# The first batch's root mean square: made compactly with tokens on partitions, spread by TensorE, its casts issued ahead of later weights' narrowing

## The chip, the core and the metric

The kernel runs on one core of one Trainium2 chip. The metric is the device time of one execution in microseconds (us). The engines are named as in the profile: PE is TensorE's matmul, PEld its weight load, DVE is VectorE, ACT is ScalarE, POOL is GpSimd, SP is SyncE.

## What is computed

Attention without a softmax, normalised by its root mean square, and two MLPs behind it. There are 8 batches, 8 heads, 576 tokens and 64 values per head; the MLPs are 512 wide with 2048 hidden values, on 4608 tokens.

```python
kv = np.einsum('bhsd,bhse->bhde', k, v)
out = np.einsum('bhsd,bhde->bhse', q, kv)
rms = np.sqrt(np.mean(out * out, axis=-1, keepdims=True) + 1e-06)
x = out / rms * g_norm            # then tokens by 512 values
h = x @ w_in;  g = 0 if h <= -1, h if h >= 1, else (h + 1)**2 / 4;  x = g @ w_out
h = x @ moe2_w_in;  g = max(h, 0)**2;  x = g @ moe2_w_out
```

## The kernel before

**Stages.** The tokens go through the first MLP in blocks of 512. The attention of the first batch (b = 0) has to come first, since nothing else can feed the first MLP; that of the later batches lies in hooks between the MLP's products. After the start TensorE works on the MLPs' products without a break to the end.

**Three products for one.** The MLPs' f32 operands are split into a rounded value and a rest, `split` (L185): a cast on ACT (the "hi") and a subtraction on DVE (the "lo"); `mm3` then makes three products. A weight tile arrives as raw words and is narrowed first, `narrow_w` (L217): one ACT operation (L224) and two DVE operations (L226, L227), then split by `split_w` (L231; L173 the cast, L187 the subtraction). The weights of the first hidden tiles, w1_0_f (in) and w1_1_f (out), are narrowed and split while the first batch's attention runs.

**The first batch's attention** treats two heads together, hp = 0 to 3, in plain f32, with a head's 64 values on 64 partitions and 576 tokens in two halves of 288:

- `kv_stage` (L396): 8 + 2 small products pkv, and two DVE copies of 64x64 to kv0 (L175).
- `t_first` (L414): q is transposed by PE into pt, and copied by DVE to qT (L175).
- `o_first` (L428): per half one product po = kv0 by qT; ACT squares it to y (L434); o = po times g, on ACT for one half (L165) and on DVE for the other (L167).
- `r_first` (L447): per half one product pr = ones by y, which puts the mean of a head's squares on all of its 64 partitions; then the reciprocal root on the full 128x576: ACT takes Ln (L455, two halves), Exp (L457) and a square (L181); DVE makes one Newton step (L441, two halves; L444) and multiplies with o (L445). POOL keeps the tokens over 512 (L464), and the rest is split into x1_0_hp (L173 on ACT, L187 on DVE).

`attention` (L522) puts these into slots of a list, and the main program goes through it by slot; `split_w` of the first six weight tiles is put in at slots SPLITS. `keep_warm` (L985) issues bf16 products of zeros, pwarm, that nothing reads. The framework's scheduler then orders the instructions by priority, which is the order in which they are written, and by what is ready.

**PSUM.** There are eight banks: two of ps_t ("at"), two of ps_h ("h"), four of ps_a ("acc0" to "acc3"). `bank` (L325) hands all eight out in turn to the first batch. Later the first MLP's ph takes "h" and its second product acc takes "acc".

**After it** the first MLP begins: `h_stage` makes ph1_0_f = w1_0_f by the four x1_0_c (12 matmuls of 128x512, L194), ACT and DVE turn ph into u and split it into gs (L571, L573), and acc follows two tiles later.

Of the kernel before, what the change touches and what calls it, by code (L numbers as in the profile page):

```python
# [44 lines left out]
    "o": "AD A A",  # L45
# [31 lines left out]
def linear_attention_rms_two_mlps(  # L77
# [12 lines left out]
    nc = tc.nc  # L90
# [80 lines left out]
    def copy(e, dst, src):  # L171
        if e is nc.scalar:
            e.copy(dst, src)  # L173
        elif e is nc.vector:
            e.tensor_copy(dst, src)  # L175
        else:
            scaled(e, dst, src, 1.0)
# [7 lines left out]
    def split(t, src, op, phase):  # L185
        copy(engine(op + "_hi", phase), t[:, 0, :], src)
        engine(op + "_lo", phase).tensor_tensor(  # L187
            t[:, 1, :], src, t[:, 0, :].bitcast(F32), ALU.subtract
        )

# [41 lines left out]
    def split_w(L, f, which):  # L232
# [7 lines left out]
        if which == 1 and f >= NF - TAIL:  # L240
            nc.sync.dma_start(wtd[f - (NF - TAIL)], t.rearrange("p a f -> p (a f)").bitcast(F32))

# [51 lines left out]
    def prep_split(which, i, n):  # L294
# [26 lines left out]
    banks = itertools.cycle(  # L321
        [(ps_t, "at")] * 2 + [(ps_h, "h")] * 2 + [(ps_a, f"acc{c}") for c in range(KD)]
    )

    def bank(b, name):  # L325

        pool, tag = next(banks) if b == 0 else (ps_t, "at")
        return pool.tile([P, TB], F32, tag=tag, name=name)

# [40 lines left out]
    def load_first():  # L370


        left = wp.tile([REM, 2, H, D], F32, tag="w0_3", name="kvr0")
        qr = wp.tile([REM, H, D], F32, tag="w1_3", name="qr0")
# [53 lines left out]
    def o_first(hp):  # L428
        qT = hl.pop((0, hp))
        y, o = scratch(hp, "y"), scratch(hp, "o")  # L430
        for half in range(2):
            ps = bank(0, f"po_0_{hp}_{half}")
# [13 lines left out]

    def r_first(hp):  # L447
        y, o = og.pop((0, hp))
        t = scratch(hp, "t")
        ms = []  # L450
        for half in range(2):
            ps = bank(0, f"pr_0_{hp}_{half}")
            m = ps[:, :U]
            nc.tensor.matmul(m, ones.bitcast(F32), y[:, half], start=True, stop=True)
            nc.scalar.activation(y[:, half], m, AF.Ln, bias=lnb, scale=LN_SCALE)  # L455
            ms.append(m)
        nc.scalar.activation(y, y, AF.Exp, bias=expb, scale=-0.5)  # L457
        square(engine("y", 0), t, y)
        for half in range(2):
            newton(t[:, half], ms[half])  # L460
        norm(t, y, o)
# [4 lines left out]
        split(x, t[:, :, :n], "x", 0)  # L466
# [451 lines left out]
    for n, (L, b) in enumerate(blocks):  # L918
# [20 lines left out]
        if n == 0:  # L939
# [3 lines left out]
            for i in range(NF - AHEAD):  # L943
                for w in range(2):
                    hook(n, i, w, split_w, 1, i + AHEAD, w)
# [32 lines left out]
    for f in range(1, 4):  # L978
# [30 lines left out]
    for i in range(2 * AHEAD):  # L1009
        first.setdefault(SPLITS[i], []).append((split_w, (1, i // 2, i % 2)))  # L1010
    for s in sorted(first):
        for f, a in first[s]:
            f(*a)
    for f in range(4, 6):
# [80 lines left out]
```

## Time and profile before

| what | us |
|---|---|
| median of three runs | 1603.74 (1602.43, 1603.74, 1603.84) |
| the profiled execution | 1603.82 |
| its span, first to last instruction | 1602.0 |
| what lies around the span | 1.82 |

The mean granted clock of TensorE over the span is 0.994 of full speed. In rows of the trace's timeline a row is one instruction or several alike on one engine: its start, the time from its start to its last end, the engine, the source line, out<-in, the shape and the count; in square brackets the idle time of that engine ahead of it, and what ended it. An f32 product is two passes of PE, and so two records; a product of split operands is one.

### The profile page before, as it was taken

Reading aid. Unit: us, or ns where it says so; the run is one execution under the profiler, and the core shown is the slowest. Engines: PE = TensorE matmul, PEld = TensorE weight load, DVE = VectorE, ACT = ScalarE, POOL = GpSimd, SP = SyncE. Lnnn points to the kernel's source line nnn. Section 1 sums busy time; section 2 is a strip of 40 time slices with the busy share of each in tenths; the row PEclk is TensorE's granted clock in tenths of the full one; section 3 lists DMA queues with packets and bytes.
Section 4 is the critical chain, followed back from the end, with each engine's and each line's share of the span. In section 5 each row is a group of like instructions: output and inputs, shape, how many; then the busy total and the mean of one; then the engine's idle time right before and its main releaser. Section 6 shows DMA issues by size and latency. Waiting matters only on the chain.

```text
span 1602.0 us, 21127 instructions
## 1 busy us (share of the span) xinstructions
PE 1582.5 (99%) x7528; PEld 1294.9 (81%) x7528; DVE 949.9 (59%) x1574; ACT 912.0 (57%) x1661; POOL 112.0 (7%) x105
## 2 busy tenths in 40 slices
PE   8899999999999999999999999999999999999998
PEld 5788888888888888888888888888888888888886
DVE  6896656666666575643244348754974496457522
ACT  5886757667666675754344466546645663664321
POOL 0000000000000000000000121012101300320000
PEclk8999999999999999999999999999999999999999
DMA  9936567576766747523141457586769676865783
GB/s 261 270 110 162 194 182 224 170 220 200 224 199 206 235 143 222 195 82 105 40 146 39 156 190 245 191 215 224 238 199 243 205 227 192 248 216 191 191 244 104
DMA packets 306969, 302.36 MB, mean 189 GB/s; under 512 B 195504, under 2 KB 248752, under 8 KB 306864
## 3 DMA queue, kind: packets, MB, share of 16 engines
q1 hardware_dynamic: 304880, 300.22, 61.5%
q8 instruction: 60, 0.98, 0.2%
q10 hardware_dynamic: 1984, 0.79, 0.2%
q14 instruction: 45, 0.37, 0.1%
HBM read 231.74 MB, written 69.21 MB: 188 GB/s over the span
## 4 chain that ended last, share of the span: by engine, by line
PE 72%; issue 15%; DVE 8%; DMA 2%; ACT 2%; POOL 1%; SPq 0%; DVEq 0%; POOLq 0%; ACTq 0%
PE acc L194 27%; PE ph L194 27%; PE ph L749 10%; PE po L749 4%; DVE t L694 3%; PE pkv L406 2%; DVE x L694 1%; PE po L194 1%; DMA xr<-x1d 1%; POOL t L810 1%; PE pr L505 1%; DVE g L839 1%; DVE xr L717 1%; DMA raw<-in_moe_w_in_dram 1%; POOL g L811 0%
## 5 line engine op out<-in xcount | busy, mean ns | idle before, releaser
L194 PE MATMUL ph<-x,w 128*128 128x512 f32 x1728 | 423.2, 393 | 5.2 <-DVE u L573 2.6
L194 PEld LDWEIGHTS ph<-x,w 128*128 128x128 f32 x1728 | 322.3, 189 | 73.3 <-DVE u L573 3.3
L749 PE MATMUL po<-t,ws 128*128 128x512 f32 x1344 | 307.4, 390 | 1.9 <-DVE t L694 1.9
L749 PE MATMUL ph<-x,ws 128*128 128x512 f32 x1344 | 306.5, 389 | 0.6 <-DVE e L794 0.6
L749 PEld LDWEIGHTS po<-t,ws 128*128 128x128 f32 x1344 | 251.5, 188 | 57.1 <-DVE t L694 5.1
L749 PEld LDWEIGHTS ph<-x,ws 128*128 128x128 f32 x1344 | 252.1, 188 | 54.1 <-DVE e L794 1.9
L194 PE MATMUL acc<-gs,w 128*128 128x512 f32 x1152 | 281.4, 391 | 0.0
L194 PEld LDWEIGHTS acc<-gs,w 128*128 128x128 f32 x1152 | 213.8, 188 | 43.5 <-ACT ev L605 0.2
L571 ACT ACTIVATE u<-ph,halfb 128x512 f32<-128x512 f32 x144 | 99.3, 690 | 196.7 <-PE ph L194 195.9
L573 DVE SCALAR_TENSOR_TENSOR u<-u,ph 128x512 f32<-128x512 f32 x144 | 98.6, 684 | 171.8 <-ACT u L181 171.3
L694 DVE TENSOR_TENSOR t<-g,t 128x512 fp32r<-128x512 f32 x192 | 134.9, 709 | 74.3 <-ACT t L173 72.3
L173 ACT CAST t<-g 128x512 fp32r<-128x512 f32 x192 | 116.5, 621 | 71.8 <-DVE t L694 51.6
L187 DVE TENSOR_TENSOR gs<-u,gs 128x512 fp32r<-128x512 f32 x160 | 110.3, 689 | 61.0 <-ACT gs L173 60.0
L173 ACT CAST gs<-u 128x512 fp32r<-128x512 f32 x160 | 99.5, 622 | 71.7 <-DVE u L573 55.3
L194 PE MATMUL acc<-gs,wt 128*128 128x512 f32 x576 | 139.4, 391 | 0.0
L194 PEld LDWEIGHTS acc<-gs,wt 128*128 128x128 f32 x576 | 106.8, 188 | 21.6
L802 DVE TENSOR_TENSOR h<-ph,e 128x512 f32<-128x512 f32 x96 | 66.1, 691 | 55.9 <-PE ph L749 50.2
L803 ACT ACTIVATE h<-h 128x512 f32<-128x512 f32 x96 | 60.5, 630 | 60.0 <-DVE h L802 56.0
L181 ACT ACTIVATE u<-u 128x512 f32<-128x512 f32 x144 | 91.0, 632 | 2.1
L810 POOL TENSOR_TENSOR t<-g 128x512 f32<-128x512 f32 x32 | 43.1, 1346 | 633.9 <-ACT g L804 353.3
L804 ACT ACTIVATE g<-h 128x512 f32<-128x512 f32 x128 | 80.9, 632 | 3.6
L794 DVE TENSOR_TENSOR e<-ph,e 128x512 f32<-128x512 f32 x64 | 43.4, 688 | 44.3 <-PE ph L749 43.3
(108 smaller groups left out, 1433.1 us busy)
## 6 DMA issues: line engine op xcount, KB each, us to landing
ws<-wsd SPq DMA_DIRECT2D x224, 512.0 KB, 3.6
wsd<-s SPq DMA_DIRECT2D x112, 256.0 KB, 3.7
wt<-wtd SPq DMA_DIRECT2D x48, 512.0 KB, 4.4
raw<-in_moe_w_in_dram SPq DMA_DIRECT2D x32, 512.0 KB, 6.0
raw<-in_moe_w_out_dram SPq DMA_DIRECT2D x32, 512.0 KB, 6.0
wcd<-s SPq DMA_DIRECT2D x32, 512.0 KB, 3.1
ws<-wcd SPq DMA_DIRECT2D x32, 512.0 KB, 3.6
x1d<-ev SPq DMA_DIRECT2D x36, 256.0 KB, 3.5
```

What stands on the lines that cost most here:

```text
L173: e.copy(dst, src)
L181: e.activation(dst, src, AF.Square)
L187: engine(op + "_lo", phase).tensor_tensor(t[:, 1, :], src, t[:, 0, :].bitcast(F32), ALU.subtract)
L194: nc.tensor.matmul(dst, wt(a), xt(c), start=first and n == 0, stop=last and n == 2)
L571: nc.scalar.activation(u, ps, AF.Relu, bias=halfb, scale=0.5)
L573: nc.vector.scalar_tensor_tensor(u, u, 1.0, ps, op0=ALU.min, op1=ALU.max)
L694: engine2(op + "_lo").tensor_tensor(t[:, 1, :], src, t[:, 0, :].bitcast(F32), ALU.subtract)
L749: nc.tensor.matmul(ps, wt(a), xt(c), start=first and n == 0 and i == 0, stop=last and n == len(lhs) - 1 and i == 2, skip_group_check=True,)
L802: nc.vector.tensor_tensor(h, bank, add, ALU.add)
L803: nc.scalar.activation(h, h, AF.Relu)
L804: nc.scalar.activation(g, h, AF.Square)
L810: engine2("t_sum").tensor_tensor(t1[k], b, a, ALU.subtract)
```

## The change

`r_first` no longer makes the reciprocal root on 128x576. It multiplies each 96 tokens of y, as the stationary operand, by two columns of ones, which gives the means with 96 tokens on partitions and 12 columns (2 halves of 3 groups of 2 heads), pm. Ln, Exp, the square and the Newton step run on 96x12. Then each column, broadcast to 64 columns as the stationary operand, is multiplied by the 96x96 identity, which spreads it over 64 partitions, pr: 12 products for a pair of heads. DVE multiplies o by pr directly out of PSUM, per half. Three bf16 products of zeros are added per pair. o is made by ACT in both halves. po takes the "acc" banks, and the turn of the other tiles goes over four banks instead of eight. `o_first` and `r_first` get a higher priority; the first weights are split in another order; and those that come last, and the hooked ones of two later tiles, may be issued only after the cast and the subtraction of the last x tile (`issue_after`). Two scratch tiles of the first loads move to other places of the weight ring, and one more pair of raw weights is loaded ahead.

```diff
-    "o": "AD A A",
+    "o": "A A A",
...
+    def split_later(*a):
+        with tc.issue_after(marks[-1][0].ins), tc.issue_after(marks[-1][1].ins):
+            split_w(*a)
...
-    banks = itertools.cycle(
-        [(ps_t, "at")] * 2 + [(ps_h, "h")] * 2 + [(ps_a, f"acc{c}") for c in range(KD)]
-    )
+    banks = itertools.cycle([(ps_t, "at")] * 2 + [(ps_h, "h")] * 2)
...
+    PT = 96
+    NPT = U // PT
...
-        left = wp.tile([REM, 2, H, D], F32, tag="w0_3", name="kvr0")
-        qr = wp.tile([REM, H, D], F32, tag="w1_3", name="qr0")
+        left = wp.tile([REM, 2, H, D], F32, tag="w0_5", name="kvr0")
+        qr = wp.tile([REM, H, D], F32, tag="w1_5", name="qr0")
...
-            ps = bank(0, f"po_0_{hp}_{half}")
+            c = 2 * (hp % 2) + half
+            ps = ps_a.tile([P, TB], F32, tag=f"acc{c}", name=f"po_0_{hp}_{half}")
...
         t = scratch(hp, "t")
-        ms = []
+        e, r = (y[:PT, i, : 4 * NPT] for i in range(2))
+        m = bank(0, f"pm_0_{hp}")[:PT, : 4 * NPT]
+        for j in range(2 * NPT):
+            nc.tensor.matmul(
+                m[:, 2 * j : 2 * j + 2],
+                y[:, j // NPT, j % NPT * PT : (j % NPT + 1) * PT],
+                ones[:, ::D].bitcast(F32),
+                start=True,
+                stop=True,
+            )
+        keep_warm(3)
+        nc.scalar.activation(e, m, AF.Ln, bias=lnb[:PT], scale=LN_SCALE)
+        nc.scalar.activation(e, e, AF.Exp, bias=expb[:PT], scale=-0.5)
+        nc.vector.tensor_tensor(r, e, e, ALU.mult)
+        newton(r, m)
+        nc.vector.scalar_tensor_tensor(r, r, -3.0, e, op0=ALU.add, op1=ALU.mult)
         for half in range(2):
             ps = bank(0, f"pr_0_{hp}_{half}")
-            m = ps[:, :U]
-            nc.tensor.matmul(m, ones.bitcast(F32), y[:, half], start=True, stop=True)
-            nc.scalar.activation(y[:, half], m, AF.Ln, bias=lnb, scale=LN_SCALE)
-            ms.append(m)
-        nc.scalar.activation(y, y, AF.Exp, bias=expb, scale=-0.5)
-        square(engine("y", 0), t, y)
-        for half in range(2):
-            newton(t[:, half], ms[half])
-        norm(t, y, o)
+            for j in range(NPT):
+                k = 2 * (NPT * half + j)
+                for h in range(2):
+                    nc.tensor.matmul(
+                        ps[h * D : (h + 1) * D, j * PT : (j + 1) * PT],
+                        r[:, k + h : k + h + 1].broadcast_to([PT, D]),
+                        ident[:PT, :PT],
+                        start=True,
+                        stop=True,
+                    )
+            nc.vector.tensor_tensor(t[:, half], o[:, half], ps[:, :U], ALU.mult)
...
-        split(x, t[:, :, :n], "x", 0)
+        marks.append(split(x, t[:, :, :n], "x", 0))
...
-                    hook(n, i, w, split_w, 1, i + AHEAD, w)
+                    later = split_later if i < 2 else split_w
+                    hook(n, i, w, later, 1, i + AHEAD, w)
...
-    for i in range(2 * AHEAD):
-        first.setdefault(SPLITS[i], []).append((split_w, (1, i // 2, i % 2)))
+    for i, (f, w) in enumerate(((0, 0), (1, 0), (0, 1), (2, 0), (1, 1), (2, 1))):
+        if i < 4:
+            first.setdefault(SPLITS[i], []).append((split_w, (1, f, w)))
+        else:
+            first.setdefault(SPLITS[-1] + 1, []).append((split_later, (1, f, w)))
     for s in sorted(first):
         for f, a in first[s]:
-            f(*a)
+            if f in (o_first, r_first):
+                with tc.high_priority():
+                    f(*a)
+            else:
+                f(*a)
```

Three places of the program show how the instructions stand now. The first is PE around the root mean square of the first pair of heads; in a name the numbers are the batch, the pair and the half, and the last one is only an allocation's, so pr_0_0_1_400 is pair 0, second half. Before:

```order
L454 MATMUL pr_0_0_1_400<-y_0_0_351,ones_198 128x288
L454 MATMUL pr_0_0_0_397<-y_0_0_351,ones_198 128x288
L433 MATMUL po_0_1_0_414<-qT_0_1_334,kv0_203 128x288
L433 MATMUL po_0_1_1_418<-qT_0_1_334,kv0_203 128x288
L406 MATMUL pkv_0_2_372<-v_0_2_234,k_0_2_232 64x64 x8
L406 MATMUL pkv_0_2_372<-kvr0_209 64x64 x2
L454 MATMUL pr_0_1_1_457<-y_0_1_412,ones_198 128x288
L422 MATMUL pt_0_2_0_386<-ident_197,q_0_2_236 128x128 x2
L424 MATMUL pt_0_2_0_386<-ident_197,qr0_210 128x32
L422 MATMUL pt_0_2_1_391<-ident_197,q_0_2_236 128x128 x2
```

After (pm_0_0 are pair 0's means, pr_0_0_0 and pr_0_0_1 its spreading):

```order
L427 MATMUL pt_0_2_0_390<-ident_197,q_0_2_236 128x128
L429 MATMUL pt_0_2_0_390<-ident_197,qr0_210 128x32
L427 MATMUL pt_0_2_1_395<-ident_197,q_0_2_236 128x128
L462 MATMUL pm_0_0_401<-ones_198,y_0_0_355 96x2 x6
L427 MATMUL pt_0_2_1_395<-ident_197,q_0_2_236 128x128
L429 MATMUL pt_0_2_1_395<-ident_197,qr0_210 128x32
L439 MATMUL po_0_2_0_515<-qT_0_2_389,kv0_203 128x288
L439 MATMUL po_0_2_1_519<-qT_0_2_389,kv0_203 128x288
L480 MATMUL pr_0_0_0_417<-ident_197,y_0_0_355 64x96 x6
L480 MATMUL pr_0_0_1_425<-ident_197,y_0_0_355 64x96 x6
L411 MATMUL pkv_0_3_453<-v_0_3_240,k_0_3_238 64x64 x8
L411 MATMUL pkv_0_3_453<-kvr0_209 64x64
```

What was two products is now six and twelve. They stand among and behind the transposes of pair 2, the spreading behind its po too, where before pr_0_0 stood ahead of po of pair 1; three pwarm stand just ahead of this stretch.

The second place is PE at the end of the first batch's attention and the start of the first MLP. Before:

```order
L454 MATMUL pr_0_2_1_490<-y_0_2_469,ones_198 128x288
L433 MATMUL po_0_3_0_504<-qT_0_3_442,kv0_203 128x288
L433 MATMUL po_0_3_1_508<-qT_0_3_442,kv0_203 128x288
L454 MATMUL pr_0_3_0_520<-y_0_3_502,ones_198 128x288
L454 MATMUL pr_0_3_1_523<-y_0_3_502,ones_198 128x288
L194 MATMUL ph1_0_0_557<-x1_0_0_286,w1_0_0_369 128x512 x3
L194 MATMUL ph1_0_0_557<-x1_0_1_287,w1_0_0_369 128x512 x3
L194 MATMUL ph1_0_1_646<-x1_0_0_286,w1_0_1_483 128x512 x3
L194 MATMUL ph1_0_1_646<-x1_0_1_287,w1_0_1_483 128x512 x3
```

After:

```order
L462 MATMUL pm_0_3_584<-ones_198,y_0_3_566 96x2 x3
L480 MATMUL pr_0_1_0_494<-ident_197,y_0_1_436 64x96
L480 MATMUL pr_0_1_1_502<-ident_197,y_0_1_436 64x96 x6
L480 MATMUL pr_0_2_0_547<-ident_197,y_0_2_513 64x96 x6
L480 MATMUL pr_0_2_1_555<-ident_197,y_0_2_513 64x96 x6
L480 MATMUL pr_0_3_0_600<-ident_197,y_0_3_566 64x96 x6
L480 MATMUL pr_0_3_1_608<-ident_197,y_0_3_566 64x96 x6
L194 MATMUL ph1_0_0_637<-x1_0_0_290,w1_0_0_373 128x512 x3
L194 MATMUL ph1_0_0_637<-x1_0_1_291,w1_0_0_373 128x512 x3
L194 MATMUL ph1_0_0_637<-x1_0_2_292,w1_0_0_373 128x512 x3
L194 MATMUL ph1_0_0_637<-x1_0_3_293,w1_0_0_373 128x512 x3
L194 MATMUL ph1_0_1_726<-x1_0_0_290,w1_0_1_450 128x512 x3
```

The 31 spreading products of pairs 1 to 3 that stand here come in one run ahead of the first ph, and the twelve matmuls of the first ph are no longer in turn with those of the second.

The third place is DVE ahead of u1_0_0, by which the first ph bank comes free. Before:

```order
L445 TENSOR_TENSOR t_0_3_519<-o_0_3_503,t_0_3_519 128x576
L227 SCALAR_TENSOR_TENSOR d1_0_2_536<-raw1_0_2_248,d1_0_2_536 128x512
L226 TENSOR_SCALAR d1_1_2_543<-raw1_1_2_250 128x512
L187 TENSOR_TENSOR x1_0_3_289<-t_0_3_519,x1_0_3_289 128x512
L187 TENSOR_TENSOR w1_0_2_539<-d1_0_2_536,w1_0_2_539 128x512
L227 SCALAR_TENSOR_TENSOR d1_1_2_543<-raw1_1_2_250,d1_1_2_543 128x512
L226 TENSOR_SCALAR d1_0_3_628<-raw1_0_3_252 128x512
L226 TENSOR_SCALAR d1_1_3_640<-raw1_1_3_254 128x512
L227 SCALAR_TENSOR_TENSOR d1_0_3_628<-raw1_0_3_252,d1_0_3_628 128x512
L187 TENSOR_TENSOR w1_1_2_546<-d1_1_2_543,w1_1_2_546 128x512
L573 SCALAR_TENSOR_TENSOR u1_0_0_570<-u1_0_0_570,ph1_0_0_557 128x512
```

After:

```order
L487 TENSOR_TENSOR t_0_3_583<-o_0_3_567,pr_0_3_1_608 128x288
L186 TENSOR_TENSOR x1_0_2_292<-t_0_2_530,x1_0_2_292 128x512
L186 TENSOR_TENSOR x1_0_3_293<-t_0_3_583,x1_0_3_293 128x512
L226 TENSOR_SCALAR d1_1_1_620<-raw1_1_1_246 128x512
L226 TENSOR_SCALAR d1_1_2_627<-raw1_1_2_250 128x512
L227 SCALAR_TENSOR_TENSOR d1_1_1_620<-raw1_1_1_246,d1_1_1_620 128x512
L227 SCALAR_TENSOR_TENSOR d1_1_2_627<-raw1_1_2_250,d1_1_2_627 128x512
L226 TENSOR_SCALAR d1_0_3_708<-raw1_0_3_252 128x512
L186 TENSOR_TENSOR w1_1_1_623<-d1_1_1_620,w1_1_1_623 128x512
L227 SCALAR_TENSOR_TENSOR d1_0_3_708<-raw1_0_3_252,d1_0_3_708 128x512
L186 TENSOR_TENSOR w1_1_2_630<-d1_1_2_627,w1_1_2_630 128x512
L599 SCALAR_TENSOR_TENSOR u1_0_0_650<-u1_0_0_650,ph1_0_0_637 128x512
```

All four x1_0 subtractions stand ahead of the narrowing of w1_1_1, w1_1_2 and w1_0_3 now, and eight operations of that narrowing (L226, L227, L186) stand between the last x1_0 and u1_0_0. On ACT, likewise, the casts of x1_0_1 to x1_0_3 stand ahead of the scaling of raw1_1_1 and of what follows it.

## Rows read from the trace of the kernel before

**Rows 1.** The page, part 1: PE's busy time, share of the span, instructions.

```profile
PE 1582.5 (99%) x7528; PEld 1294.9 (81%) x7528; DVE 949.9 (59%) x1574; ACT 912.0 (57%) x1661; POOL 112.0 (7%) x105
```

**Rows 2.** Timeline of PE at the first MLP's start (start us, us, operation, idle before).

```profile
32.32 4.72 PE L194 MATMUL ph<-x,w 128*128 128x512 f32 x12
37.21 1.92 PE L194 MATMUL ph<-x,w 128*128 128x512 f32 x6 [0.17 <-ACT x L173]
41.33 0.73 PE L194 MATMUL ph<-x,w 128*128 128x512 f32 x2 [2.21 <-ACT x L173]
42.26 1.52 PE L194 MATMUL ph<-x,w 128*128 128x512 f32 x4 [0.20 <-DVE x L187]
46.39 1.22 PE L194 MATMUL ph<-x,w 128*128 128x512 f32 x2 [2.61 <-DVE u L573]
...
48.80 2.99 PE L194 MATMUL ph<-x,w 128*128 128x512 f32 x10
51.63 2.88 PE L194 MATMUL acc<-gs,w 128*128 128x512 f32 x12
54.35 2.88 PE L194 MATMUL ph<-x,w 128*128 128x512 f32 x12
```

**Rows 3.** Windows: each engine's busy us (instructions), granted clock, DMA share, GB/s.

```profile
36.10:42.90 6.80, 4.23 (x15) 2.21 (x15) 6.75 (x14) 5.63 (x10) 1.27 (x2) 1.00 0.87 225
42.95:49.75 6.80, 4.19 (x27) 2.58 (x26) 6.02 (x12) 5.87 (x12) 0.00 (x0) 0.50 0.88 186
...
19.00:32.30 13.30, 11.64 (x52) 7.20 (x53) 9.73 (x22) 8.48 (x19) 0.48 (x2) 0.74 0.83 257
```

**Rows 4.** Timeline of PE before 19 us, at the full clock, and at 18.97.

```profile
6.73 1.47 PE L988 MATMUL pwarm<-warm 128*128 128x512 bf16 x6
...
9.27 0.38 PE L422 MATMUL pt<-ident,q 128*128 128x128 f32 x2
...
10.30 0.69 PE L406 MATMUL pkv<-v,k 128*64 128x64 f32 x16
...
11.18 1.24 PE L433 MATMUL po<-qT,kv 128*128 128x288 f32 x4
...
13.94 1.13 PE L454 MATMUL pr<-y,ones 128*128 128x288 f32 x4
14.91 1.13 PE L433 MATMUL po<-qT,kv 128*128 128x288 f32 x4
...
18.97 1.27 PE L454 MATMUL pr<-y,ones 128*128 128x288 f32 x2 [1.75 <-ACT y L434]
```

**Rows 5.** Timeline of DVE: the second raw weight tile's narrowing.

```profile
16.20 0.69 DVE L227 SCALAR_TENSOR_TENSOR d<-raw,d 128x512 int32<-128x512 int32 x1 [0.46 <-ACT raw L224]
```

**Rows 6.** Groups by form, 19 to 46.4 us: shapes, count | busy us, mean ns | idle.

```profile
L441 DVE SCALAR_TENSOR_TENSOR t<-pr,t 128x288 f32<-128x288 f32 x7 | 3.1, 449 | 0.0
L444 DVE SCALAR_TENSOR_TENSOR t<-t,y 128x576 f32<-128x576 f32 x4 | 3.0, 753 | 0.0
L445 DVE TENSOR_TENSOR t<-o,t 128x576 f32<-128x576 f32 x4 | 3.0, 750 | 0.0
L455 ACT ACTIVATE y<-pr,lnb 128x288 f32<-128x288 f32 x6 | 2.9, 502 | 2.3 <-PE pr L454 2.3
...
L457 ACT ACTIVATE y<-y,expb 128x576 f32<-128x576 f32 x3 | 2.3, 766 | 0.0
...
L181 ACT ACTIVATE t<-y 128x576 f32<-128x576 f32 x3 | 2.0, 671 | 0.0
```

**Rows 7.** Timeline of PEld: two weight loads of po with nothing between them.

```profile
11.18 0.30 PEld L433 LDWEIGHTS po<-qT,kv 128*128 128x128 f32 x2
```

**Rows 8.** Tile po: duration ns of one (min/median/max), first and last start.

```profile
L433 PEld LDWEIGHTS po<-qT,kv x16: 186/190/337, 11.2 to 28.9; 128*128 128x128 f32 x16
```

**Rows 9.** Tile pkv, the same columns.

```profile
L406 PE MATMUL pkv<-v,k x64: 222/222/369, 6.1 to 25.7; 128*64 128x64 f32 x64
...
L175 DVE COPY kv<-pkv x8: 205/222/229, 10.2 to 26.5; 64x64 f32<-64x64 f32 x8
```

More of the change, by code (lines that the diff above doesn't have):

```diff
@@ L172, in copy @@
         if e is nc.scalar:
[L173 to L177, printed above, removed]
+            return e.copy(dst, src)
+        if e is nc.vector:
+            return e.tensor_copy(dst, src)
+        return scaled(e, dst, src, 1.0)
     def square(e, dst, src):
@@ L185, in split @@
     def split(t, src, op, phase):
-        copy(engine(op + "_hi", phase), t[:, 0, :], src)
-        engine(op + "_lo", phase).tensor_tensor(
+        hi = copy(engine(op + "_hi", phase), t[:, 0, :], src)
+        lo = engine(op + "_lo", phase).tensor_tensor(
             t[:, 1, :], src, t[:, 0, :].bitcast(F32), ALU.subtract
         )
+        return hi, lo
     def mm3(dst, wt, xt, first, last):
@@ L445, in norm @@
         nc.vector.tensor_tensor(t, o, t, ALU.mult)
+    marks = []
     def r_first(hp):
@@ L977, in linear_attention_rms_two_mlps @@
     load_first()
-    for f in range(1, 4):
+    for f in range(1, 5):
         for w in range(2):
@@ L1008, in linear_attention_rms_two_mlps @@
         first[s].append((keep_warm, (n,)))
-    for i in range(2 * AHEAD):
-        first.setdefault(SPLITS[i], []).append((split_w, (1, i // 2, i % 2)))
+    for i, (f, w) in enumerate(((0, 0), (1, 0), (0, 1), (2, 0), (1, 1), (2, 1))):
[3 more added lines that the diff above has]
+            first.setdefault(SPLITS[-1] + 1, []).append((split_later, (1, f, w)))
     for s in sorted(first):
         for f, a in first[s]:
-            f(*a)
-    for f in range(4, 6):
+            if f in (o_first, r_first):
[3 more added lines that the diff above has]
+                f(*a)
+    for f in range(5, 6):
         for w in range(2):
```

## The prediction

> **What bounds the kernel now.** First the page's list of busy time: PE is busy 99% of the span [rows 1], so time can be won or lost only where PE waits, runs at the lower clock, or gets other work. Then PE's timeline at the start of the first MLP [rows 2], the last place where this change touches anything: from 51.63 on, 12 matmuls take 2.72 us (51.63 to 54.35), 0.227 each, without a break, and all later work follows at that pace. So the whole effect is a shift of that stream. Its size is best told by an *equivalent start*, the moment from which a stream at full pace without waits would reach the same point: 36 ph matmuls (12 + 6 + 2 + 4 + 2 + 10) and one pkv group lie between 32.32 and 51.63; at full pace they need 36 x 0.227 = 8.2 and 0.88 (a pkv group at full clock, from 10.30 to 11.18 [rows 4]), so the equivalent start is 51.63 - 9.1 = 42.6. The first ph stands at 32.32. Of the 10.3 us lost in between, four waits take 0.17 + 2.21 + 0.20 + 2.61 = 5.2 [rows 2], for casts and subtractions of x and for u. The rest is the clock: twelve ph matmuls took 4.72, 0.39 each [rows 2], and the granted clock goes between full (1.00 from 36.1 to 42.9, 2.4 GHz) and half (0.50 from 42.95 to 49.75, 1.2 GHz) [rows 3]. Over the attention itself, 19.0 to 32.3, it is 0.74 on average, with PE busy 11.64 of 13.30 us [rows 3].
>
> **What the change removes.** Per pair ACT loses two Ln of 0.502, an Exp of 0.766 and a square of 0.671, 2.44 us; DVE loses two operations of 0.449, one of 0.753, one of 0.750, 2.40 us [rows 6], and one o of 128x288, which ACT takes over (about 0.5, like the Ln of the same shape). The new operations on 96x12 are not in the trace: two on ACT and three on DVE per pair, each between nothing and the 0.222 of a 64x64 copy [rows 9]; I take the 0.222, the smallest of DVE here. DVE gets two products of 128x288, 0.449 each as the same shape reading PSUM [rows 6]. Net per pair: ACT 2.44 - 0.44 - 0.5 = 1.5 less, DVE 2.9 - 0.67 - 0.9 = 1.3 less; over four pairs 6 and 5 us. All of this lies beside PE. It is worth something only as far as PE waits for these engines, and that is at most the 5.2 us of [rows 2].
>
> **What it adds on PE,** where nothing covers it once PE has no waits. Up to about 19 PE is held in both kernels: before by y until 18.97 [rows 4]; after, because the first pwarm of pair 0 takes the PSUM bank of pkv of pair 2, and the two copies that free it stand on DVE behind the subtraction of w1_1_0. That weight's second narrowing step ran at 16.20 after a wait for ACT [rows 5]; with 0.69 for it and as much each for cast and subtraction the chain ends at 18.2 if ACT gives it the same moment, and up to 1.9 later with the o and y operations that now stand ahead on ACT. I take 19.0, with both ends within 1 us.
>
> From there to the first ph PE has, at full clock:
> - transposes of pairs 2 and 3: 1.03 a pair (9.27 to 10.30 [rows 4]), 2.06;
> - po of two pairs: 0.97 each (four passes of 128x288 from 13.94 to 14.91), 1.94; pkv of one pair, 0.88 [rows 4];
> - twelve pwarm: 1.47 for six, 0.245 each [rows 4], 2.94;
> - pm: 24 products, 48 passes. Such a pass loads 96 columns and streams two, which no row shows. From below a pass is 0.031, that of pkv (sixteen in 0.69, one of them 0.222, so (0.69 - 0.222)/15 [rows 4, 9]), 1.5 in all. From above it is 0.17, the mean of the six passes of a pair's transposes, which load 128 columns and fewer and change shape (1.03/6 [rows 4]), 8.2 in all. Nearest is the bare load of 128 columns: two in 0.30, one of them 0.19, so 0.11 apart [rows 7, 8]; by 96/128 this is 0.083, 3.98;
> - pr: 48 products, 96 passes of 96 columns into 64 partitions. I take pkv's pace by its columns, 0.031 x 96/64 = 0.046, 4.42; below, 0.031 a pass, 3.0; above, without passes side by side, po's 0.28 (1.13 for four [rows 4]) x 96/288 = 0.094, 9.0;
> - about ten changes of shape: a pkv group takes 0.88 and its 20 passes at 0.031 are 0.62, so its two changes cost 0.26, 0.13 each, 1.30.
>
> Sum 17.5 us. The work is of the kind that ran at a mean clock of 0.74 [rows 3], so it lasts 17.5/0.74 = 23.7. To this come 1.2 of waits: the last pair's spreading waits for Ln, Exp and three DVE operations with two products of 0.449 between them on DVE, of which some 2 us of earlier spreading hides the most; 0.9 is left, and 0.3 for the rest. The first ph comes at 19.0 + 23.7 + 1.2 = 43.9, where it was 32.32.
>
> **On a rule of the skill.** The sixteen passes of pkv, all over the same 128 rows, follow at 0.031 [rows 4, 9], less than the 0.055 that 64 columns need by the bare loads (0.11 for 128 [rows 7, 8]): loads ran under other passes. The Trainium skill, page "TensorE: Matmul & The Clock Gate", Part 3, The mechanism, says in the list there that a weight load overlaps with products in flight only where its row group differs. By that rule pr, whose passes share their rows, would pay its loads too, and the sum would be 22.8 instead of 17.5.
>
> **What follows after the first ph.** The first ph takes a bank of ps_h that the last pr held, so it waits for a DVE product, 0.449 and a hand-over, 0.7. The third hidden tile waits for u1_0_0, with eight narrowing operations ahead of it on DVE that before were spread over earlier time: the same wait was 2.61 [rows 2]; between 0 and that I take 1.2. The stream starts at half clock with some chance: twelve matmuls at half cost 4.72 - 2.72 = 2.0 [rows 2]; half of that, 1.0. The 5.2 us of waits for x go, as four x tiles are ready in order by then. Equivalent start: 43.9 + 0.7 + 1.2 + 1.0 = 46.8, against 42.6: 4.2 later. The change breaks even with the first ph at 39.7.
>
> **Costed at nothing:** the moved scratch tiles and the earlier loads on SP's queue, since no wait in [rows 2] was ended by a DMA; without that cover, a late raw tile would push the narrowing and so u. POOL's copy is as before. The later narrowing of w1_1_1 (first used by acc) is hidden by the three ph tiles ahead of it.
>
> The profiled execution took 1603.82, its span 1602.0 and 1.82 around it, 0.08 above the median of 1603.74; I add to the former. **Forecast: 1603.82 + 4.2 = 1608.0.**
>
> **The rivals.**
> - *The clock holds* (0.18). The twelve pwarm and a PE without pauses keep full clock. For it: where PE ran without a break, after 51.63, it did; against it: from 19.0 PE was busy 88% and still had 0.74 [rows 3]. First ph at 19.0 + 17.5 + 1.2 = 37.7, equivalent start 39.6, which is 3.0 earlier: 1600.8.
> - *PE is not what is late* (0.12). pm and pr are both near their lower ends and overlap, the first ph comes about when it did, and the relief of ACT and DVE takes away the waits of [rows 2]: at the most 5.2, 1598.6. It decides as long as the first ph stands before about 37. For it: 5.2 us are shown; against it: PE's own sum is 13.6 even with both at their lower ends.
> - *pm is cheap* (0.10). At pkv's 0.031 it needs 2.5 less, 3.4 at clock 0.74: 1604.6.
> - *The clock stays lower* (0.12). Loads and short passes get a mean of 0.60: 17.5/0.60 = 29.2, 5.5 more: 1613.5. Spreading without passes side by side gives about the same, 4.6/0.74 = 6.2 more: 1614.2.
> - *Each spreading pass pays its load* (0.03). 64 columns by the row of bare loads, 0.055 x 96 = 5.3, at 0.74 7.1: 1615.1. This is the page's rule above; pkv's 0.031 speaks against it.
> - That the change does not do what it says I give nothing: the order shows the compact form and the x casts ahead of the narrowing.
>
> **How the numbers follow.** The forecast has 0.45, with 1604 to 1612 as its own range (0.5 to 1 us each way for the start at 19, the clock between 0.70 and 0.80, u's wait between its ends). About 0.2%, 3.2 us, is what a measurement of this kernel can tell from no change, so same lies between 1600.5 and 1606.9. Faster: all of "PE is not late" (0.12) and 0.07 of "the clock holds", 0.19. Same: 0.11 of that, "pm is cheap" 0.10 and 0.14 of the forecast, 0.35. Slower: 0.31 of the forecast, 0.12 and 0.03, 0.46. The range goes from 1599.0 to 1612.5; half of "PE is not late" and most of the two slow cases stay outside, under 0.2.
>
> **What would show it.** In the timeline of PE: the first ph near 44 and no wait for x of over 0.5 us after it; pm 0.08 and pr 0.046 from pass to pass at full clock; pwarm of pair 0 at 19. In the windows: a granted clock near 0.74 from 19 to 44. In the waits: PE waiting for u once, about 1 us. I am wrong if the first ph comes before 39.7, if the clock is 1.00 throughout, or if PE still waits for ACT and DVE while pm and pr stand idle behind them.

## The result

| | kernel before | changed kernel |
|---|---|---|
| median of 20 runs, us | 1602.61 | 1612.88 |
| lowest to highest, us | 1599.94 to 1603.84 | 1603.20 to 1615.88 |
| ratio to before | | 1.0061, 95% interval 1.0053 to 1.0069 |
| profiled execution: time, span, us | 1603.82, 1602.0 | 1613.25, 1611.4 |
| mean granted clock over the span | 0.994 | 0.990 |

The changed kernel is slower by 0.6%, 9.8 us of 1603. The forecast was 4.2 us slower: the direction is right, the size is less than half of what came, and 1612.88 lies 0.4 us above the upper end of the forecast's range, 1612.5.

The page of the changed kernel, parts 1 and 2 (busy time; granted clock in tenths by 40 slices):

```profile
PE 1596.9 (99%) x7668; PEld 1306.4 (81%) x7668; DVE 942.6 (58%) x1574; ACT 907.0 (56%) x1657; POOL 113.5 (7%) x105
...
PEclk7899999999999999999999999999999999999999
```

PE is as busy as before, 99% [rows 1], and the first slice of the clock, 40 us long, reads 7, where it reads 8 before. Its timeline from 19 us to the first acc (start, time to the last end, operation, idle before):

```profile
18.79 0.81 PE L1015 MATMUL pwarm<-warm 128*128 128x512 bf16 x3 [1.51 <-DVE kv L175]
...
19.98 1.67 PE L462 MATMUL pm<-ones,y 128*96 128x2 f32 x12
...
24.35 2.19 PE L480 MATMUL pr<-ident,y 96*64 96x96 f32 x24
...
27.52 1.18 PE L462 MATMUL pm<-ones,y 128*96 128x2 f32 x12
28.63 0.33 PE L411 MATMUL pkv<-kvr 64*64 64x64 f32 x2
...
31.06 2.05 PE L462 MATMUL pm<-ones,y 128*96 128x2 f32 x12
32.97 1.01 PE L1015 MATMUL pwarm<-warm 128*128 128x512 bf16 x2
...
41.02 3.46 PE L480 MATMUL pr<-ident,y 96*64 96x96 f32 x38
45.20 2.19 PE L480 MATMUL pr<-ident,y 96*64 96x96 f32 x24 [0.72 <-DVE y L474]
47.32 10.36 PE L194 MATMUL ph<-x,w 128*128 128x512 f32 x36
57.61 0.69 PE L411 MATMUL pkv<-v,k 128*64 128x64 f32 x16
...
58.34 1.89 PE L194 MATMUL acc<-gs,w 128*128 128x512 f32 x7
```

The reader is to see three things here. PE waits until 18.79 for a DVE copy (1.51 us), and once more for 0.72; there is nothing else. The first ph comes at 47.32, 15 us later than in [rows 2], and then 36 ph run without a wait. And the same product has two paces: twelve passes of pm take 1.11 us at 27.52 (until 28.63) and 1.91 at 31.06 (until 32.97). The windows of the changed kernel say which clock was granted where (length; busy us of PE, PEld, DVE, ACT, POOL; then the clock, the DMA share, GB/s):

```profile
19.00:47.30 28.30, 27.43 (x195) 20.56 (x193) 10.97 (x33) 9.56 (x23) 2.19 (x3) 0.58 0.76 239
20.40:27.10 6.70, 6.70 (x54) 5.33 (x54) 1.77 (x6) 2.19 (x7) 0.00 (x0) 0.50 1.06 374
27.20:30.50 3.30, 3.30 (x29) 2.35 (x25) 1.46 (x5) 1.64 (x4) 0.14 (x1) 1.00 1.01 383
30.60:51.00 20.40, 19.54 (x116) 14.74 (x116) 10.68 (x28) 8.72 (x19) 2.59 (x3) 0.50 0.57 143
51.10:60.00 8.90, 8.90 (x56) 6.92 (x55) 7.38 (x16) 7.66 (x16) 0.00 (x0) 1.00 0.99 334
```

From 30.6 to 51.0 the clock is at half, 1.2 GHz, and PE is busy 19.54 of these 20.40 us. From 19.0 to 47.3 DVE is busy 10.97 and ACT 9.56 of 28.3 us, and PE waits for them 0.72: the relief lands where nothing needs it.

How much of the loss up to the first acc is the clock can be worked out. The same windows of the kernel before, beside [rows 3], and then the whole stretch from 19 us to the first acc, before and after:

```profile
19.00:25.80 6.80, 6.80 (x30) 4.29 (x30) 4.48 (x10) 3.45 (x8) 0.24 (x1) 0.50 0.95 309
25.90:32.70 6.80, 5.14 (x25) 3.24 (x24) 5.51 (x13) 5.33 (x12) 0.24 (x1) 1.00 0.72 209
32.70:36.10 3.40, 3.40 (x9) 2.60 (x9) 3.40 (x7) 3.40 (x8) 0.00 (x0) 0.50 1.00 348
...
19.00:51.60 32.60, 25.76 (x108) 16.49 (x109) 28.00 (x57) 23.91 (x47) 1.75 (x4) 0.74 0.88 249
```

```profile
19.00:58.34 39.34, 38.48 (x251) 29.10 (x249) 20.43 (x51) 18.75 (x40) 2.82 (x4) 0.65 0.78 240
```

Before, PE is busy 6.80 + 3.40 + 4.19 = 14.4 us at half clock, which costs 7.2; after it is 6.70 + 19.54 = 26.2, which costs 13.1, so 5.9 more. The waits go from 6.8 to 0.9, 6.0 less. What is left of PE's busy time, its work at full clock, goes from 18.6 to 25.4, 6.8 more. The sum is the 6.7 by which the first acc comes later: at the same clock, added work and removed waits would nearly cancel.

### The profile page after: what moved, and what is told of

Its sections match the earlier page's. It is cut to its first block, busy times and chain, and to the rows that moved or that the text cites. A ratio compares the mean times of both kernels' runs of the same rounds, so it can differ in the third digit from the quotient of the medians.

```text
span 1611.4 us, 21425 instructions
## 1 busy us (share of the span) xinstructions
PE 1596.9 (99%) x7668; PEld 1306.4 (81%) x7668; DVE 942.6 (58%) x1574; ACT 907.0 (56%) x1657; POOL 113.5 (7%) x105
## 4 chain that ended last, share of the span: by engine, by line
PE 72%; issue 15%; DVE 8%; DMA 2%; POOL 1%; ACT 1%; SPq 0%; DVEq 0%; POOLq 0%; ACTq 0%
PE ph L194 27%; PE acc L194 26%; PE ph L775 10%; PE po L775 4%; DVE t L720 3%; DVE x L720 2%; PE po L194 1%; PE pkv L411 1%; POOL t L836 1%; PE pr L531 1%; DMA raw<-in_moe_w_in_dram 1%; DVE g L865 1%; DVE xr L743 1%; PE pr L480 1%; DMA xr<-x1d 1%
## 5 line engine op out<-in xcount | busy, mean ns | idle before, releaser
L186 DVE TENSOR_TENSOR gs<-u,gs 128x512 fp32r<-128x512 f32 x160 | 110.3, 689 | 63.8 <-ACT gs L173 62.6
L820 DVE TENSOR_TENSOR e<-ph,e 128x512 f32<-128x512 f32 x64 | 43.4, 688 | 44.3 <-PE ph L775 43.3
```

Source lines behind the costliest of these rows:

```text
L186: lo = engine(op + "_lo", phase).tensor_tensor(t[:, 1, :], src, t[:, 0, :].bitcast(F32), ALU.subtract)
```

## The experiments

Three theories were set against each other. **A**: the amount of PE's work between 19 us and the first ph, over the granted clock, sets the end. **B**: the new order (priorities, marks, four banks) costs the time, not the compact form. **C** and **D**: what PE does there sets the granted clock, and the clock sets the time; C says products in PE's waits hold it up, D that the many short passes pull it down. The runs were made in three groups (e, f and g, h), each beside runs of the kernel before, with medians of 1602.7 to 1602.8; the changed kernel itself was not run again beside them.

| kernel | median us (runs) | ratio to before, 95% | first ph at | mean clock, 19 to first ph |
|---|---|---|---|---|
| changed | 1612.88 (20) | 1.0061 (1.0053 to 1.0069) | 47.3 | 0.58 |
| e1_no_warm | 1605.67 (11) | 1.0019 (1.0010 to 1.0028) | 44.0 | 0.58 |
| e2_full_form | 1601.38 (11) | 0.9988 (0.9979 to 0.9996) | 39.0 | 0.84 |
| e3_compact_only | 1601.87 (11) | 1.0011 (0.9991 to 1.0031) | 31.5 | 1.00 |
| e4_wide_spread | 1612.01 (6) | 1.0053 (1.0040 to 1.0065) | 45.9 | 0.60 |
| f1_no_priority | 1601.85 (11) | 0.9994 (0.9985 to 1.0002) | 38.9 | 0.86 |
| f3_before_warm | 1598.40 (6) | 0.9971 (0.9959 to 0.9983) | 31.7 | 1.00 |
| f4_compact_no_warm | 1606.24 (11) | 1.0024 (1.0015 to 1.0034) | 41.5 | 0.65 |
| g1_pm_dense | 1606.91 (12) | 1.0016 (1.0005 to 1.0028) | 45.8 | 0.68 |
| h1_full_order_warm | 1607.63 (5) | 1.0036 (1.0023 to 1.0049) | 43.5 | 0.79 |
| h2_noprio_dense | 1600.10 (11) | 0.9990 (0.9981 to 0.9999) | 36.3 | 1.00 |
| h3_before_warm5 | 1599.02 (11) | 0.9978 (0.9969 to 0.9987) | 34.9 | 0.89 |
| h5_warm_acc | 1604.73 (11) | 1.0011 (1.0002 to 1.0019) | 43.4 | 0.61 |

First ph and clock are those of the one profiled execution of each kernel; the times scatter around it.

**Without the pwarm of r_first.**

```diff
-        keep_warm(3)
```

> The changed kernel without the three pwarm products of each pair in r_first. In the changed kernel's trace PE has no wait from 18.8 to 47.3 but one of 0.7 us, at a mean granted clock of 0.58. Theory A (PE's work from 19 us to the first ph sets the end, by its amount at full clock over the granted clock): twelve pwarm are 12 x 0.245 = 2.9 us at full clock, 5.1 at 0.58, so the first ph comes near 42.2 and the time is about 5 us under the changed kernel's, 1608. Theory B (the loss comes from the new order: priorities, marks, four banks): PE only waits where the pwarm were, the first ph stays at 46 to 47 and the time within 1.5 us of the changed kernel's. Theory C (the pwarm hold the clock up): without them the mean clock falls towards 0.50, 13.1/0.50 = 26 instead of 28 us, about 1 to 2 us under the changed kernel's, with hardly a stretch at full clock between 19 and 45.

The time fell by 7 us. The window of this kernel from 19 us to its first ph:

```profile
19.00:44.00 25.00, 21.41 (x178) 17.43 (x177) 12.73 (x37) 9.40 (x23) 1.11 (x3) 0.58 0.89 279
```

The clock is the same 0.58, so in the profiled executions, which lie 5.8 us apart, the twelve pwarm neither hold it up nor pull it down; they are work, as A says. Over all executions the median of the span's mean clock is 0.992 against 0.990, so a small pull is not ruled out. A's 5 us and first ph at 42.2 were 2 us off in both: PE has new waits for DVE's compact results, 3.2 us in place of 0.7, the 1.5 us of wait for pwarm's bank is gone, and v came 1.2 us later from the DMA. C, 1 to 2 us, and B, none, fall for this place.

**The old form in the new order,** and **the new form in the old order.** In the first, `r_first` has its old body (ones by y, Ln, Exp, square, Newton on 128x576) and all else is the changed kernel; in the second, the kernel before has the new body and nothing else.

```diff
 e2_full_form, against the changed kernel:
-        m = bank(0, f"pm_0_{hp}")[:PT, : 4 * NPT]
...
+            nc.tensor.matmul(m, ones.bitcast(F32), y[:, half], start=True, stop=True)
...
+        norm(t, y, o)
```

> The changed kernel with the old r_first (ones by y, Ln, Exp, square and Newton on 128x576); all the rest of the change kept: priorities, marks, order of the weights, four banks, po in the acc banks, o on ACT. Theory A: from 19 us PE has transposes 2.1, po 1.9, pkv 0.9 and pr 4 x 0.97 = 3.9, 8.8 us at full clock, well under 12 at a clock of 0.74, so PE is not the bound; first ph at 31 to 35, then waits for x as in the kernel before; the time is near the kernel before's, 1600 to 1605, 8 to 12 us under the changed kernel's. Theory B (the order costs it): within 3 us of the changed kernel's, 1610 to 1615.

```diff
 e3_compact_only, against the kernel before:
-            nc.tensor.matmul(m, ones.bitcast(F32), y[:, half], start=True, stop=True)
...
+        m = bank(0, f"pm_0_{hp}")[:PT, : 4 * NPT]
...
+        keep_warm(3)
...
+            nc.vector.tensor_tensor(t[:, half], o[:, half], ps[:, :U], ALU.mult)
```

> The kernel before with the compact r_first alone (pm, three pwarm, 96x12, spreading), in the old order, with eight banks and without priorities and marks. Theory A: PE has the same 17.5 us at full clock from about 19 on as in the changed kernel, so the first ph comes at 42 to 48 and the time is 5 to 11 us over the kernel before's, 1607 to 1614. Theory B (the order costs it): within 3 us of the kernel before's.

At the median neither half alone costs anything: the order with the old form is 0.1% faster than before, the compact form in the old order cannot be told from before. That the loss needs both does not follow: two of the eleven executions of the compact form in the old order took 1614.7 and 1615.2 us, the whole loss. B falls with the first (it would have 1610 to 1615); the first ph came at 39.0 there, later than A's 31 to 35, after a wait of 3.8 us for DVE's t. But A falls with the second in the form that was expected, too: PE has the same products, and yet ph begin at 31.5, among the last compact products, and the last spreading stands at 37.6, not at 42 to 48. Its timeline, at the start of the first MLP, and its window:

```profile
30.10 1.10 PE L457 MATMUL pm<-ones,y 128*96 128x2 f32 x12
31.06 0.81 PE L1009 MATMUL pwarm<-warm 128*128 128x512 bf16 x3
31.52 0.58 PE L194 MATMUL ph<-x,w 128*128 128x512 f32 x1
31.93 0.66 PE L457 MATMUL pm<-ones,y 128*96 128x2 f32 x6
32.45 1.63 PE L194 MATMUL ph<-x,w 128*128 128x512 f32 x6
34.02 1.21 PE L475 MATMUL pr<-ident,y 96*64 96x96 f32 x24
```

```profile
19.00:31.50 12.50, 12.02 (x123) 9.02 (x126) 8.80 (x22) 6.38 (x17) 1.01 (x2) 1.00 0.84 263
```

Here the clock was granted in full throughout, 1.00 with PE busy 12.02 of 12.50 us. Full clock is not certain with this kernel: the eleven times go from 1599.8, at a mean clock of 0.999 over the span, to 1615.2 at 0.989, with the same instructions in the same order. So the compact form's work on PE costs nothing against the kernel before at the full clock and 12 us at a poor one. The difference of 0.010 in the clock, over 1600 us, is 16 us, and the times differ by 15.3.

**One wide product for six short ones in the spreading.** This kernel leaves out the spreading of each root to its own tokens, so x has other values.

```diff
-            for j in range(NPT):
-                k = 2 * (NPT * half + j)
-                for h in range(2):
...
+            nc.tensor.matmul(
+                ps[:, :U],
+                r[:, half : half + 1].broadcast_to([PT, P]),
+                o[:PT, half],
```

> The changed kernel with the spreading of a half done by one product, a column of the compact result broadcast to 96x128 by 96x288 of o, instead of six of 96x64 by 96x96: the values are wrong, the place, the waits and DVE's products are the same. At full clock 16 passes of 0.24 are 3.9 us instead of the 4.4 forecast for 96 short passes. Theory A with a clock that does not depend on the kind of work: about 0.5/0.58 = 1 us under the changed kernel's, the mean clock from 19 to the first ph 0.55 to 0.62. Theory D (the many short products between 31 and 47 are what PE did while the clock stayed at half): with wide ones the clock rises to 0.70 or more, 16/0.74 = 21.6 instead of 27.6, 5 to 7 us under the changed kernel's.

The window of this kernel where the changed one has half clock:

```profile
31.10:48.00 16.90, 16.43 (x51) 11.42 (x52) 8.12 (x23) 6.63 (x16) 1.51 (x3) 0.50 0.69 171
```

It is at half there too, and the time fell by 1 us, as A has it. D falls for the spreading: its short passes are not what brings the clock down.

**Without the higher priority.**

```diff
-            if f in (o_first, r_first):
-                with tc.high_priority():
-                    f(*a)
-            else:
-                f(*a)
+            f(*a)
```

> The changed kernel without the higher priority of o_first and r_first; all else as changed. Theory A (PE's amount of work over the granted clock): PE has the same work between 19 and the first ph, in nearly the same order; the first ph stays at 45 to 48, the time within 2 us of the changed kernel's 1612. Theory B2 (the priority, with the compact form, keeps the first MLP's matmuls out of PE's pauses): several ph stand ahead of the last spreading, 1603 to 1608.

A expected 2 us and 11 came. PE's order is nearly the same, and no ph stands ahead of the last spreading, so the rival's mechanism is not what happened either. What differs most is the clock; the windows of this kernel:

```profile
19.60:22.90 3.30, 3.08 (x10) 1.75 (x10) 1.92 (x6) 1.20 (x5) 0.00 (x0) 0.50 1.00 270
23.00:36.50 13.50, 11.69 (x146) 8.90 (x147) 9.90 (x27) 8.01 (x20) 1.24 (x3) 1.00 1.03 366
36.70:43.40 6.70, 6.57 (x35) 5.45 (x36) 4.11 (x9) 3.41 (x6) 0.24 (x1) 0.50 0.79 157
```

There is half clock for two short stretches, and full clock in the 13.5 us in which most of the compact work lies; in the changed kernel that work lay in the 20 us at half. The eleven times go from 1599.3 at 0.998 to 1604.2 at 0.996.

**Pwarm in the kernel before.**

```diff
             ms.append(m)
+        keep_warm(3)
         nc.scalar.activation(y, y, AF.Exp, bias=expb, scale=-0.5)
```

> The kernel before with three pwarm products of zeros per pair behind pr, and no other edit. It asks whether products without meaning hold the granted clock up where PE would otherwise wait. Theory A (they are work like any other, 2.9 us at full clock, of which the 1.7 us of waits before 19 and others hide some): mean clock from 19 to 49.75 stays at 0.70 to 0.78, time 0 to 3 us over the kernel before's. Theory C (they hold the clock): mean clock 0.90 or more there, the half-clock loss of some 5 us goes, 1597 to 1600.

As C has it: 1598.4, the lowest median of all kernels here, 0.3% faster than the kernel before and 0.9% faster than the changed one, and its six times lie within 0.9 us. The clock from 19 to 49.75 us is 0.94, where C asked for 0.90. Its windows:

```profile
19.00:36.10 17.10, 13.53 (x69) 7.63 (x69) 16.37 (x36) 15.24 (x31) 1.58 (x3) 1.00 1.05 355
36.20:39.50 3.30, 3.30 (x8) 2.63 (x9) 3.30 (x6) 2.81 (x5) 0.63 (x1) 0.50 0.72 134
39.60:50.00 10.40, 8.92 (x56) 6.98 (x56) 10.18 (x21) 8.13 (x16) 0.00 (x0) 1.00 0.85 228
```

Where the kernel before has 0.74 [rows 3], this one has 1.00. But the pwarm do not simply fill PE's waits. Their rows around 19 us, where the kernel before falls to half clock after a wait of 1.75 us [rows 4], and the window up to the first ph:

```profile
14.73 0.81 PE L989 MATMUL pwarm<-warm 128*128 128x512 bf16 x3
...
18.75 1.24 PE L454 MATMUL pr<-y,ones 128*128 128x288 f32 x4 [0.74 <-DVE t L441]
```

```profile
19.00:31.75 12.75, 10.65 (x60) 6.10 (x61) 12.21 (x27) 10.89 (x23) 0.87 (x2) 1.00 1.03 356
```

The work ahead of this pr stands later, by 0.5 us for the pwarm at 14.73 and by 0.3 for a v that the DMA brings later, and pr itself comes 0.2 earlier, so the wait is 0.74, and the clock stays full. Behind it PE is busy 10.65 of 12.75 us, 84%, where the kernel before, at 0.74, had 88% [rows 3]: what goes with the full clock here is the shorter wait ahead of 19 us, not a fuller PE behind it. Each keep_warm also takes a bank in the turn and shifts the order of what follows; that was not tested apart. Twelve products that nothing reads are worth 4.3 us.

**The compact form alone, without its pwarm.** The edit is that of the first experiment, on e3_compact_only.

> The kernel before with the compact r_first alone, as in the earlier run with only the compact form, but without the three pwarm per pair. There the eleven times went from 1599.8 at a mean clock of 0.999 to 1615.2 at 0.989. Theory A: 2.9 us less of PE's work; at full clock 1597 to 1600, and the slowest executions 4 to 6 us better than 1615. Theory C (the pwarm keep the clock at full in the good executions): without them most executions have a clock of 0.993 or less and the median is over 1604.

As C has it again: the clock is 0.990 to 0.994 over the span in all eleven executions, and the median is 4.4 us over that with the pwarm. So in the old order the pwarm of the compact form hold the clock in most executions; in the new order (e1) they did not. Short waits alone do not hold it either: in the profile of this kernel the clock is at half from 18 to 28 us, though PE's waits in the 3 us ahead of that were 0.4 and 0.5.

**64 columns streamed in pm instead of two.**

```diff
-        m = bank(0, f"pm_0_{hp}")[:PT, : 4 * NPT]
+        mw = bank(0, f"pm_0_{hp}")[:PT, : 2 * NPT * D]
+        m = mw[:, :: D // 2]
...
-                m[:, 2 * j : 2 * j + 2],
+                mw[:, D * j : D * (j + 1)],
...
-                ones[:, ::D].bitcast(F32),
+                ones[:, ::2].bitcast(F32),
```

> The changed kernel with 64 columns of ones (every second of the 128) as moving operand of pm instead of two; the same means come out, each 32 times. A pass still loads 96 columns, 0.083 us at full clock as measured in the changed kernel's trace (1.18 us for twelve, one of them about 0.25), and streams 64 columns, which pkv's passes do in 0.031 or less, so its time should hardly change: Theory A: first ph within 1.5 us of 47.3, time within 2 us of the changed kernel's 1612. Theory D2 (PE at weight loads with next to nothing streamed is what stands ahead of the low clock): the mean clock from 19 to the first ph rises from 0.58 to 0.70 or more, and the time falls by 5 us or more, to 1607 or less.

For D, in pm: 6 us less for 32 times as many columns streamed, though twelve passes take about as long as before (1.23 at full clock, 1.18 with two columns). The time is what D2 forecast, the clock with 0.68 a little under its 0.70. The windows of this kernel:

```profile
20.80:37.80 17.00, 16.36 (x97) 12.93 (x96) 6.93 (x20) 5.90 (x16) 0.37 (x1) 0.50 0.88 304
37.90:51.00 13.10, 12.68 (x115) 9.23 (x115) 8.18 (x22) 7.23 (x16) 0.71 (x3) 1.00 0.60 129
```

The clock came back at 37.8 instead of 51, with 12 of the 48 passes of pm, 7 of the 12 pwarm and 72 of the 96 passes of the spreading still ahead. The edit also moved pm, pwarm and po among each other on PE, so the columns are not tested alone. In two of its twelve executions the clock over the span was 1.00, and the time 1600.2 and 1600.4.

**Both: no priority and 64 columns,** the two edits above together.

> The changed kernel without the higher priority and with 64 columns of ones streamed in pm: the two edits that each brought the changed kernel down, 10 and 5 us, both by a higher granted clock. If the clock is the whole cause, both together end at a clock of 0.998 or more and at the lowest times that either reached, 1598.5 to 1600.5; if the two have different causes that add, under 1597; if the clock was chance, 1601 to 1607.

The window from 19 us to the first ph, of this kernel:

```profile
19.00:36.20 17.20, 15.07 (x181) 10.98 (x179) 12.55 (x35) 9.17 (x23) 1.32 (x3) 1.00 1.01 342
```

Full clock and 1600.1, as the clock as the one cause has it; 12.8 us under the changed kernel with the same number of products. The compact form then beats the kernel before, by 0.1%, and not the kernel before with pwarm. What the 64 columns add to the missing priority is not clear: the interval, 0.9981 to 0.9999, overlaps that of f1_no_priority, 0.9985 to 1.0002.

**Three further runs.** The old form in the new order, with pwarm behind pr:

> The changed kernel with the old r_first on 128x576 (as in the earlier run with the full form, 1601.4) and three pwarm products behind pr of each pair. In that run the clock was at half from 18.3 to 25.1 and from 38.8 to 42.2, and PE waited 3.8 us for the last x. Theory C (pwarm in PE's waits hold the clock): about half of the lost 5 us comes back, 1597 to 1600, and the times scatter by less than 1.5 us. Theory A: 12 more products of 0.245, most of them in waits, 1601 to 1604.

Both theories had it at 1604 or less; it gave 1607.6, and the mean clock was 0.79 where it is 0.84 without the pwarm, so C fails here. Its waits on PE:

```profile
PE pr L462 <- DVE kv L175: 3.0, 2, 1.6
PE pr L462 <- DVE t L447: 2.6, 1, 2.6
...
PE po L439 <- DVE qT L175: 1.6, 2, 1.0
```

In e2_full_form the same view has 1.9, 1.3 and, for qT (there ahead of pr), 1.1. Products meant to fill waits made them longer; that it is their share of the four banks, which DVE frees late, is likely and was not tried. Five pwarm instead of three in the kernel before:

> The kernel before with five pwarm behind pr of each pair instead of three (three gave 1598.4 at 0.999). With the clock full already, eight more products of 0.22 are either hidden in waits or cost up to 1.8 us: 1598 to 1600. If the clock was still lost in places (0.5 from 36.1 to 39.6 in the run with three), 1597 to 1598.

1599.0: within the first case of what was expected, no better than three. And the pwarm of the changed kernel in banks that are free early:

> The changed kernel with the pwarm of r_first in the acc banks, which are free early. The scheduler then issues most of them before 17 us, and PE does not stand from 17.3 to 18.8 behind a bank that DVE frees. Theory A: nine pwarm less between 19 and the first ph, 2.2 us at full clock, 3.8 at 0.58, and the 1.5 us of that wait: first ph near 42, 1606 to 1608. If it was that wait which let the clock fall for so long, the clock is 0.996 or more and the time 1600 to 1603, as without the priority; if the pwarm among pm and the spreading held up what clock there was, 1610 or more.

1604.7 lies between A's 1606 to 1608 and the 1600 to 1603 for the wait as the cause: taking the wait at 17.3 away is not enough by itself. The clock from 19 to the first ph is 0.61.

**The clock over all executions.** Of the 222 timed executions of the fourteen kernels, the time goes with the mean clock of the span with a correlation of -0.90 (for the twenty of the changed kernel -0.95). Medians of the time by that clock: 1613.2 us for those under 0.9905 (22 of them), 1606.2 up to 0.9935 (38), 1603.0 up to 0.9965 (99), 1600.9 up to 0.9985 (42), 1599.0 above (21).

## Why the prediction was right and where it was not

**What bounds the kernel: right for most of it.** PE has no wait for x in the changed kernel. The shift of the ph stream was to be the whole effect; it is 6.7 of the 9.4 us by which the span grew: 36 ph and a pkv group before 58.34 (9.05 us at full pace) make an equivalent start of 49.3, 6.7 later than the 42.6 of before; 46.8 was forecast.

**The hold until 19: right,** place and mechanism: pwarm of pair 0 starts at 18.79, after 1.51 us for the copy of kv.

**The sum of PE's work: its list right, its size 1.6 us too large.** PE is busy 27.43 us at a clock of 0.58, which is 15.9 at full clock; 17.5 was forecast. The waits are 0.9, with 1.2 forecast; 0.72 of it is at the place that was named, the last pair's spreading. The two products that no row showed were priced well: pm at full clock is 1.11 for twelve with a change of shape in it, (1.11 - 0.13)/12 = 0.082, forecast 0.083. The spreading is 0.047 a pass where it ran at full clock (24 passes from 32.22 to 33.35 in f1_no_priority), forecast 0.046; its loads ran under other passes as those of pkv do, and the rival in which each spreading pass pays its load would have given 0.10. A pwarm was taken at 0.245, and three in a row take 0.65, 0.217 each (25.37 to 26.02 in h2_noprio_dense), which makes 0.3 of the 1.6; the rest was not followed up.

The spreading's full-clock rows, from the timeline of f1_no_priority:

```profile
32.22 1.21 PE L480 MATMUL pr<-ident,y 96*64 96x96 f32 x24
33.35 1.18 PE L462 MATMUL pm<-ones,y 128*96 128x2 f32 x12
```

**The granted clock: wrong, and the step that failed.** The sum was divided by 0.74, because the work is "of the kind that ran at a mean clock of 0.74". But that mean is no property of the work: it is one stretch at 0.50, to 25.8, and one at 1.00, from 25.9 on, in one order of one kernel. The changed kernel's work ran at 0.58. Alone this would have made 17.5/0.58 = 30.2 of the 23.7, and the first ph would have come at 50.4 instead of 43.9. It came at 47.3: the work, 1.6 too large in the sum, gave back 2.8 and the waits 0.3. That the first ph is only 3.4 later than forecast is luck. These 3.4 are part of the 5.2 us by which the profiled execution (9.4 us over before in span) lies above the forecast.

The rival "the clock stays lower", with 0.60, had the clock and was given 0.12; that its 1613.5 also meets the time is luck, as its sum is too large by the same 1.6 and it has nothing for what comes behind the first acc. The rival of a full clock, 1600.8, is what the same form gave with two edits more: h2_noprio_dense 1600.1, and the one execution of the changed kernel with a clock of 0.997 took 1603.2. Both levels were in the text; what decides between them was not, and the runs show it only in part.

**After the first ph: three terms wrong, and one missing.** The wait of 0.7 for the bank and of 1.2 for u did not come, since at half clock the ph stream is slow enough for DVE; in g1_pm_dense, where it starts at full clock, PE waits 0.7 for u. The half clock at its start was 1.0 and is 10.3 - 8.2 = 2.1 (36 ph from 47.32 to 57.61). That is 0.8 less than forecast together, and the first acc stands 6.7 us later than before. The other 2.7 of the 9.4 come after it, where the forecast had nothing, and part of them is the narrowing that was moved behind the x casts. The waits of PE and of its loads there, in the changed kernel:

```profile
PE po L194 <- ACT qT L173: 0.7, 1, 0.7
```

```profile
PEld po L194 <- ACT qT L173: 1.8, 3, 1.1
...
PEld ph L194 <- ACT w L173: 0.9, 3, 0.3
```

On ACT the cast that ends the wait of po stands behind that of a late weight tile:

```profile
66.56 0.62 ACT L173 CAST w<-d 128x512 fp32r<-128x512 f32 x1
67.25 0.67 ACT L173 CAST qT<-qf 128x576 fp32r<-128x576 f32 x1
```

The shift against the kernel before grows from 6.8 us at the fourth u (57.35 and 64.12) to 8.9 at the 23rd (174.1 and 183.0); 0.7 of this is the row on PE, up to 0.9 the last row, in which the loads of ph wait for weights. The rest was not traced to single waits.

**The relief of ACT and DVE: right** that it counts only where PE waits for them. The waits for x went as forecast, but PE came to x 15 us later and would have waited less in any case, so what the relief is worth here is not shown.

**What stays open.** Why the priority costs so much clock is not isolated. It holds PE at 17.3, and it moves pwarm ahead of other work; taking pwarm out (e1) or moving it (h5) left the clock at 0.58 and 0.61, 64 columns in pm gave 0.68, and only taking the priority away raised it to 0.86. That pm's narrow stream is part of the cause is what g1 points to, with some of PE's order changed as well; it is not all of it, since f1 has the narrow pm too. PE's wait for v from the DMA, at 16 to 17 us, differs between the profiled executions (0.2 us before, 0.7 in the changed kernel, 1.9 in e1_no_warm, 2.5 in h1_full_order_warm); whether such a difference early on decides about the clock behind it was not looked at, with one profile of each kernel.

## What to carry to other kernels

Where a kernel's start is made of small products, ask first which clock they will be granted, and price the change at both levels; a work sum at a mean clock from another order of the same work is a guess. Products that nothing reads can be worth more than shortening the work of the engines that PE waits for (4.3 us here), but their place decides: in another order they cost time, so look at the banks that they take and at what a priority does to them. Take many executions: one profile of such a start shows one of its clocks. A reordering that removes a wait early sends its work later: look for who waits there.

## What was not expected of the hardware

The granted clock can stay at half while PE is busy: 0.50 from 30.6 to 51.0 in the changed kernel, PE busy 19.54 of 20.40 us. The Trainium skill, page "TensorE: Matmul & The Clock Gate", part 1, HAM oscillation, puts such losses down to PE's idle gaps; f3_before_warm agrees with that as far as the wait of PE ahead of 19 us goes (0.74 instead of 1.75 us, and a clock of 1.00 instead of 0.74 behind it), the changed kernel's 20 us at half do not.

With the same instructions in the same order the clock differed from execution to execution by up to 0.010 of the span, and the time by 15 us (e3_compact_only). What PE streams seems to count, not only that it is busy: pm with 64 columns instead of two took no longer and, with some of PE's order changed too, brought the clock of the changed kernel from 0.58 to 0.68, its median down by 6 us.
